# A decode block on one core: fewer TensorE products, and two rows of w2 loaded in two transfers

## The chip, the cores and the metric

The kernel runs on one core of a Trainium2 chip. The metric is the device time of one execution in microseconds, as the median of several runs. A profile of one further execution gives its span (from the first to the last instruction) and what each engine and each DMA queue did in it.

## The reference

One token of a transformer block is decoded for a batch of 4. The input `x` is 4 x 1 x 512; there are 32 heads of 128, a cache of 4096 keys and values per head and batch row, and a feed-forward part of width 1792. All data is float32.

```python
xn = _layernorm(x, axis=-1)                                  # no weights
q = (xn @ wq).reshape(B, Sq, H, Dh).transpose(0, 2, 1, 3)
scores = jnp.einsum("bhqd,bhkd->bhqk", q, k_cache) * (Dh ** -0.5)
p = softmax(scores, axis=-1)
o = jnp.einsum("bhqk,bhkd->bhqd", p, v_cache)
attention = o.transpose(0, 2, 1, 3).reshape(B, Sq, H * Dh) @ wo
h = silu(xn @ w1)
return x + attention + h @ w2
```

The two caches are 256 MiB each; `wq` and `wo` are 8 MiB each, `w1` and `w2` 3.5 MiB each. Every byte is read once.

## The kernel before

**Work and buffers.** A block `i` of 32 is four heads of one batch row: 8 MiB of keys and 8 MiB of values, each one DMA of 128 partitions by 64 KiB (partition `p` holds 128 positions of head `p // 32`). There are three buffers of 8 MiB: `kb[0]` and `kb[1]` for keys, `vb` for values. At the start `kb[1]` also holds `w1`, `x` and small tiles (`early`), and `vb` holds `wq`. At the end `vb` holds `wo`, and `kb[1]` holds `w2` and small tiles (`late`).

**Order.** Everything is written out by hand. Each engine has its own instruction stream, and the class `Queue` counts what an engine has done: `done` raises the engine's semaphore, `wait` makes another engine wait for a count. `load` (line 163 in the trace) issues a DMA and returns what its landing will count. SP issues all the large loads in one order: `w1`, `wq`, the keys of block 0; the keys of block 1 when `h` is out of `kb[1]`; the values of block 0 when the query projection has read `wq` out of `vb` (`p_q`); then keys and values by turns, each when its buffer is free (`k_free`, `v_free`); the last values into `kb[0]`; `wo` in two halves into `vb`; `w2` in five pieces into `kb[1]`. ACT issues the load of `x` and the store of the output.

**Start.** VectorE computes the layer norm. TensorE puts `x` into the accumulator `acc` (`accumulate`, line 239), transposes the normed rows into `xpad`, which is padded to 32 columns, and multiplies by `w1` (line 259) and `wq` (line 273). ACT applies silu, VectorE transposes `h` into `hT` (line 267). The queries are scaled (line 279), spread over the partitions by 32 small products with `heads` (line 286), and copied into `q_col` (line 295).

**Loop.** For each block VectorE multiplies keys by the query (line 358) and adds up halves that GpSimd has added (lines 378 and 353), and finds the smallest per head; ACT takes exponentials and their sums (line 390); TensorE multiplies by the values into `o_ps` (`values`, line 408), ACT copies (line 398), and `collect` (line 419) puts the result into column `i` of `o_t`.

**End.** When the last values are collected, VectorE multiplies the sums by `quad` (line 444), four products with `ones` add them up (line 455), and their reciprocal `rl` is taken (line 461). `o_t` is transposed (line 464), permuted by a product (line 468), and multiplied by `rl` into `xo`, padded to 32 columns (line 474). 32 products with `wo` go into `ow`, 512 columns wide, in four strips of 32 rows by turns (line 487). A row `f` of `w2` means 512 columns for each of the 128 partitions; there are 14 rows, and the first 7 go into `ow` the same way (line 493). ACT copies `ow` to `os` (line 498). Rows 7 to 13 go into `acc` in four products of 128 columns each (`accumulate`), and four products with `pick` add the strips of `os` to it. The last row comes in two halves (`sides`); after each half two blocks of `acc` are done and are copied out by ACT (line 517) and VectorE (line 522). The pieces of `w2` are set by these lines:

```python
W2_CUTS = (7, 11)                       # rows 0-6, 7-10, 11-12, then the two halves of row 13
f_edges = (0, *W2_CUTS, FC - 1)
for name, a, z in zip(("wq", "w2a", "w2b"), f_edges[:-1], f_edges[1:]):
    got_w2.append(load(sp, name, w2_t[:, a:z], w2_p[:, a:z], (k_free, T)))
```

Of the kernel before, what the change touches and what calls it, by code (L numbers as in the profile page):

```python
# [15 lines left out]
G = 4  # L16
# [3 lines left out]
W2_CUTS = (7, 11)  # L20
# [25 lines left out]
def kernel(  # L46
# [11 lines left out]
    nc = tc.nc  # L58
# [13 lines left out]
    scale = float(Dh) ** -0.5  # L72
    xf = x.rearrange("b s d -> (b s) d")
# [20 lines left out]
    q_all = small([P, NQ, G, Dh], "q_all")  # L94
    heads = small([P, NQ, 4, NQ, B], "heads")
# [6 lines left out]
    quad = small([P, G, 4], "quad")  # L102
    perm = small([P, P], "perm")
    ones = small([P, 1], "ones")
    rl = small([P, B], "rl")
    nmean = small([B, 1], "nmean")
    var = small([B, 1], "var")
    rstd = small([B, 1], "rstd")
    t1 = small([B, 1], "t1")
# [16 lines left out]
    x_sb, xc, sq, xn = (early[:B, at + n * D : at + (n + 1) * D] for n in range(4))  # L126
    h_sb = early[:, at + 4 * D : at + 4 * D + FJ]
# [4 lines left out]
    lt = late[:, FC * D : (FC + 1) * D].rearrange("p (b n g) -> p b n g", b=B, n=N)  # L132
    y_t = late[:, (FC + 1) * D : (FC + 1) * D + P].rearrange("p (b h) -> p b h", b=B)
    xo = late[:, (FC + 4) * D : (FC + 4) * D + PH * PH].rearrange("p (r m) -> p r m", r=PH)
# [8 lines left out]
    with tc.tile_critical():  # L143
# [5 lines left out]
        names = ["x", "w1", "wq", "k0", "k1", "v", "v_last", "w2a", "w2b", "w2c", "w2d"]  # L149
# [11 lines left out]
        def load(q, name, to, of_, *needs):  # L161
            q.wait(*needs)
            q.eng.dma_start(to, of_).then_inc(landed[name], 16)  # L163
            loads[name] += 1
            return landed[name], 16 * loads[name]
# [3 lines left out]
        got_x = load(act, "x", x_sb, xf)  # L169
# [14 lines left out]
        nc.vector.memset(xpad, 0.0).then_inc(s_free, 1)  # L184
        nc.vector.memset(q_col[:, T:, :], 0.0).then_inc(s_free, 1)
        nc.vector.memset(heads, 0.0)
# [38 lines left out]
        for u in range(NQ):  # L225
            t = nc.vector.tensor_copy(
                heads[:, u, :, u, :], ident.rearrange("p (j e) -> p j e", j=4)[:, :, :B]
            )
        d_pick = dve.done(
            nc.vector.tensor_reduce(  # L230
                quad,
                ident.rearrange("p (g m) -> p g m", g=G)[:, :, None, :].to_broadcast([P, G, 4, PH]),
                axis=AX, op=ALU.add,
            )
        )
# [10 lines left out]
        pe.wait(c_ident, got_x)  # L246
        accumulate(ident[:B, :B], x_sb, start=True)
        pe.wait(d_xn)
        xt = ps_b[:, : DC * B].rearrange("p (c b) -> p c b", c=DC)
        xn_c = xn.rearrange("b (p c) -> b c p", c=DC)  # L250
        for c in range(DC):
            t = nc.tensor.transpose(xt[:, c, :], xn_c[:, c, :], ident[:B, :B])
        p_xt = pe.done(t)
        dve.wait(p_xt)
        d_xpad = dve.done(nc.vector.tensor_copy(xpad[:, :, :B], xt))
# [12 lines left out]
        pe.wait(got_wq)  # L268
        for c in range(DC):
            for j in range(4):  # L270
                for u in range(NQ):
                    h = HJ * j + G * u
                    t = nc.tensor.matmul(  # L273
                        ps_q[32 * j : 32 * j + 32, u, :], xpad[:, c, :],
                        wq_t[:, c, h * Dh : (h + G) * Dh], start=(c == 0), stop=(c == DC - 1),
                    )
        p_q = pe.done(t)
        dve.wait(p_q)
        d_q = dve.done(nc.vector.tensor_scalar_mul(  # L279
                q_all.rearrange("p u g d -> p (u g d)"), ps_q.rearrange("p u n -> p (u n)"), -scale,  # L280
            ))
        pe.wait(d_q, d_pick)
        for g in range(G):
            for a in range(4):
                for u in range(NQ):
                    t = nc.tensor.matmul(
                        ps_b[32 * g : 32 * g + 32, 32 * a : 32 * a + 32],
                        q_all[:, u, g, 32 * a : 32 * a + 32],
                        heads[:, u].rearrange("p j v b -> p (j v b)"),
                        start=(u == 0), stop=(u == NQ - 1),  # L290
                    )
        p_col = pe.done(t)
        dve.wait(p_col)
        d_col = dve.done(
            nc.vector.tensor_copy(q_col[:, :T, :], ps_b.rearrange("p (a i) -> p i a", a=4))
        )


        got_k[1] = load(sp, "k1", kb[1], cache(k_cache, 1), p_h, d_h, p_xt)
# [17 lines left out]
        for name, a, z in zip(("wq", "w2a", "w2b"), f_edges[:-1], f_edges[1:]):  # L317
            got_w2.append(load(sp, name, w2_t[:, a:z], w2_p[:, a:z], (k_free, T)))
# [109 lines left out]
        with nc.tensor.Fori(0, T - 1) as i:  # L428
# [4 lines left out]
        take(nc.tensor, weights_ready)  # L433
# [3 lines left out]
        p_o = v_free, T  # L437


        pool.wait((k_free, T))  # L440
        c_xo = pool.done(nc.gpsimd.memset(xo, 0.0))
        dve.wait((v_free, T))
        d_lt = dve.done(
            nc.vector.tensor_tensor(  # L444
                lt,
                sums.rearrange("p (n b) -> p b n", b=B)[:, :, :, None].to_broadcast([P, B, N, G * 4]),
                quad.rearrange("p g q -> p (g q)")[:, None, None, :].to_broadcast(
                    [P, B, N, G * 4]
                ),
                op=ALU.mult,  # L450
            )
        )
        pe.wait(d_lt)
        for b in range(B):
            t = nc.tensor.matmul(
                ps_a[:, b : b + 1],
                lt[:, b].rearrange("p n g -> p (n g)"), ones, start=True, stop=True,
            )
        p_l = pe.done(t)
        dve.wait(p_l)  # L460
        d_rl = dve.done(nc.vector.reciprocal(rl, ps_a[:, :B]))
        dve.wait(p_o)
        d_y = dve.done(
            nc.vector.transpose(y_t, o_t.rearrange("p (n b) g -> p b n g", b=B))
# [4 lines left out]
                ps_b, perm, y_t.rearrange("p b r -> p (b r)"), start=True, stop=True,  # L469
            )  # L470
        )
        dve.wait(p_x, d_rl, c_xo)
        d_x = dve.done(
            nc.vector.tensor_tensor(
                xo[:, :, :B], ps_b.rearrange("p (b r) -> p r b", b=B),
                rl[:, None, :].to_broadcast([P, PH, B]), op=ALU.mult,
            )
        )
# [3 lines left out]
        pe.wait(d_x)  # L482
        for n, (a, z) in enumerate(zip(edges[:-1], edges[1:])):
            pe.wait(got_wo[n])
            for r in range(a, z):
                j = 32 * (r % 4)
                nc.tensor.matmul(
                    ow[j : j + 32, :], xo[:, r, :], wo_t[:, r, :], start=(r < 4), stop=False
                )
        pe.wait(d_h, got_w2[0])  # L490
        for f in range(f_edges[1]):
            j = 32 * (f % 4)
            t = nc.tensor.matmul(
                ow[j : j + 32, :], hT[:, f, :], w2_t[:, f, :], start=False,
                stop=(f >= f_edges[1] - 4),
            )
        act.wait(pe.done(t))
        a_os = act.done(nc.scalar.activation(os, ow, AF.Copy))
        for n, (a, z) in enumerate(zip(f_edges[1:-1], f_edges[2:])):
            pe.wait(got_w2[n + 1])  # L500
            for f in range(a, z):
                accumulate(hT[:, f, :B], w2_t[:, f, :])
            if n == 0:
                pe.wait(a_os)
                accumulate(pick[:, :B], os)


        for n, side in enumerate(sides):
            j = 2 - 2 * n
            pe.wait(got_side[n])  # L510
            p_acc = pe.done(
                accumulate(hT[:, FC - 1, :B], w2_t[:, FC - 1, :], stop=True, blocks=(j, j + 1))
            )
# [7 lines left out]
            d_out = dve.done(  # L521
                nc.vector.tensor_copy(  # L522
                    res[:, (j + 1) * P : (j + 2) * P], acc[32 * (j + 1) : 32 * (j + 1) + B, :]
                )
            )
# [35 lines left out]
```

## Time and profile before

| | |
|---|---|
| median of 3 runs | 1302.8 us (1302.73 to 1303.46) |
| profiled execution: time | 1303.4 us |
| profiled execution: span | 1300.5 us |
| busy: PE, DVE, ACT, POOL | 361.1, 964.9, 110.2, 580.9 us |
| DMA | 561.07 MB, mean 431 GB/s |
| mean granted TensorE clock | 0.623 |

In the profile PE is TensorE's products and PEld its weight loads, DVE is VectorE, POOL is GpSimd, SP issues DMAs, and L163 is line 163 of the kernel. A product in float32 appears as two MATMUL records. The granted clock is the TensorE clock that the throttle let through, as a share of full speed. The DMA share is the mean busy share of the core's 16 DMA engines; a DMA is cut into packets, and a packet of 4 bytes closes an engine's part of a transfer. A row of the timeline has start, duration, engine, line, operation, tiles and count, and in brackets the idle time before it and what ended it.

### The profile page before, as it was taken

To read this page: it belongs to the slowest core of one execution; us is meant where nothing else is said; L and a number is where in the kernel's file an instruction comes from. 1 tells how busy PE (TensorE), PEld (TensorE's weight loads), DVE (VectorE), ACT (ScalarE), POOL (GpSimd) and SP (SyncE) were. 2 spreads that over 40 slices of the span, in tenths; PEclk is the share of its full clock that TensorE was granted. 3 is DMA by queue.
4 is the path that set the end of the run, shared out by engine and by line. 5 is a ranking of instruction groups with operands and counts; after the bars stand their busy time and mean duration, and the time that the engine had idled before them with its cause. 6 is when DMAs were issued, how large, how long until landed. Compare 5 with 4: busy or idle time off the path is not lost. (4 is left out here: it accounts for less than half of the span.)

```text
span 1300.5 us, 7378 instructions
## 1 busy us (share of the span) xinstructions
PE 361.1 (28%) x2628; PEld 113.3 (9%) x2628; DVE 964.9 (74%) x449; ACT 110.2 (8%) x311; POOL 580.9 (45%) x137
## 2 busy tenths in 40 slices
PE   2221233321233221123322132332123332113337
PEld 0100001000000000000000000100000000001002
DVE  2499877887777887777797777788777788777770
ACT  1010101001010100101000010100101010010100
POOL 0255534554444554443555443455444455444350
PEclk8755666655666655666665566665566665566668
DMA  9999999999999999999999999999999999999998
GB/s 403 450 422 440 429 441 427 435 435 423 447 423 447 423 445 425 441 429 439 427 437 433 425 445 423 447 423 447 423 443 427 439 429 441 427 431 439 423 433 358
DMA packets 10533, 561.07 MB, mean 431 GB/s; under 512 B 1176, under 2 KB 1432, under 8 KB 1568
## 3 DMA queue, kind: packets, MB, share of 16 engines
q1 hardware_dynamic: 10512, 560.99, 99.6%
q8 instruction: 3, 0.05, 0.0%
q10 hardware_dynamic: 16, 0.02, 0.0%
q14 instruction: 2, 0.02, 0.0%
HBM read 561.00 MB, written 0.01 MB: 431 GB/s over the span
## 5 line engine op out<-in xcount | busy, mean ns | idle before, releaser
L378 POOL TENSOR_TENSOR k<-k 128x2048 f32<-128x2048 f32 x128 | 578.7, 4532 | 676.8 <-POOLq L326 676.8
L358 DVE TENSOR_TENSOR k<-k,q_b 128x4096 f32<-128x4096 f32 x128 | 562.4, 4414 | 226.2 <-DVEq L326 226.1
L408 PE MATMUL o_ps<-v,p_t 128*16 128x512 f32 x1984 | 285.0, 739 | 867.1 <-PEq L326 867.1
L353 DVE TENSOR_REDUCE s<-k 128x32 f32<-128x2048 f32 x128 | 290.8, 2272 | 17.9 <-DVEq L326 17.9
L408 PEld LDWEIGHTS o_ps<-v,p_t 128*16 128x16 f32 x1984 | 67.1, 113 | 1059.2 <-issue 1059.2
L398 ACT ACTIVATE o_sb<-o_ps 128x512 f32<-128x512 f32 x32 | 19.1, 597 | 1010.2 <-ACTq L326 1010.2
L329 DVE COPY q_of<-q_col 128x4 f32 (+1 forms) x33 | 84.8, 2571 | 0.0
L390 ACT ACTIVATE p_t<-s,gm 32x128 f32<-32x128 f32 x128 | 65.9, 515 | 46.0 <-ACTq L326 43.9
L419 PE MATMUL o_t<-pick,o_sb 128*128 128x4 f32 x256 | 33.6, 254 | 33.3 <-PEq L326 33.3
L419 PEld LDWEIGHTS o_t<-pick,o_sb 128*128 128x128 f32 x256 | 31.0, 191 | 62.6 <-issue 62.6
L390 ACT ACT_TABLE_LOAD x16 | 20.5, 1283 | 98.4 <-ACTq L326 98.4
L390 ACT ACTIVATION_READ_ACCUMULATOR p_t<-s,gm x128 | 24.9, 195 | 0.0
L279 DVE TENSOR_SCALAR q_all<-ps_q 128x1024 f32<-128x1024 f32 x1 | 1.2, 1224 | 20.6 <-PE ps_q L273 20.6
L444 DVE TENSOR_TENSOR k<-sums,quad 128x512 f32<-128x512 f32 x1 | 0.7, 693 | 19.0 <-PE o_t L419 19.0
L333 DVE STREAM_TRANSPOSE q_b<-q_of 128x128 f32<-128x128 f32 x33 | 10.8, 327 | 4.9
L367 DVE TENSOR_REDUCE m<-s 128x1 f32<-128x128 f32 x32 | 9.2, 286 | 4.7
L273 PE MATMUL ps_q<-v,xpad 128*32 128x512 f32 x64 | 8.8, 706 | 13.3 <-DMA v<-in_A_wq_dram 13.3
L408 PE MATMUL o_ps<-k,p_t 128*16 128x512 f32 x64 | 9.5, 757 | 8.3 <-DMA k<-in_A_v_cache_dram 8.3
L369 DVE STREAM_TRANSPOSE mt<-m 128x32 f32<-128x32 f32 x32 | 6.8, 212 | 4.7
L522 DVE COPY k<-acc 4x128 f32<-4x128 f32 x2 | 0.6, 286 | 12.5 <-PE acc L239 12.5
L371 DVE TENSOR_REDUCE gm<-mt 128x1 f32<-128x32 f32 x32 | 6.0, 186 | 4.7
L267 DVE STREAM_TRANSPOSE hT<-k 128x448 f32<-128x448 f32 x1 | 0.9, 939 | 10.3 <-ACT k L265 10.3
(62 smaller groups left out, 54.1 us busy)
## 6 DMA issues: line engine op xcount, KB each, us to landing
v<-in_A_wo_dram SPq DMA_DIRECT2D x2, 4096.0 KB, 27.2
k<-in_B_w_dram SPq DMA_DIRECT2D x1, 3584.0 KB, 11.2
k<-in_B_w_dram SPq DMA_DIRECT2D x1, 1792.0 KB, 30.3
k<-in_B_w_dram SPq DMA_DIRECT2D x1, 1024.0 KB, 32.4
k<-in_A_k_cache_dram SPq DMA_DIRECT2D x32, 45.4
k<-in_B_w_dram SPq DMA_DIRECT2D x1, 512.0 KB, 33.2
v<-in_A_v_cache_dram SPq DMA_DIRECT2D x31, 27.2
k<-in_B_w_dram SPq DMA_DIRECT2D x2, 128.0 KB, 33.0
```

The lines of the kernel that those rows point to most:

```text
L273: t = nc.tensor.matmul(ps_q[32 * j : 32 * j + 32, u, :], xpad[:, c, :], wq_t[:, c, h * Dh : (h + G) * Dh], start=(c == 0), stop=(c == DC - 1),
L329: nc.vector.tensor_copy(q_of, q_col[:, at, :].rearrange("p i g -> p (i g)")).then_inc(spread_done, 1)
L333: nc.vector.transpose(q_b[:, n, :], q_of[:, :, None].to_broadcast([P, G, PH])).then_inc(spread_done, 1)
L353: nc.vector.tensor_reduce(s[:, a:z], k[:, a:z, : Dh // 2], axis=AX, op=ALU.add).then_inc(summed, 1)
L358: nc.vector.tensor_tensor(k[:, a:z, :], k[:, a:z, :], q_b[:, n, None, :].to_broadcast([P, z - a, Dh]), op=ALU.mult,).then_inc(products, 1)
L367: nc.vector.tensor_reduce(m_t, s, axis=AX, op=ALU.min).then_inc(summed, 1)
L369: nc.vector.transpose(mt, m_t.to_broadcast([P, PH])).then_inc(summed, 1)
L378: nc.gpsimd.tensor_tensor(kb[n][:, a:z, : Dh // 2], kb[n][:, a:z, : Dh // 2], kb[n][:, a:z, Dh // 2 :], op=ALU.add,).then_inc(halves, 1)
L390: t = nc.scalar.activation(p_t[rows, :, g], s_t[n][rows, :], AF.Exp, bias=gm[n][rows, :], scale=-1.0, accum_out=sums[rows, bass.ds(i * 2 + ...
L398: nc.scalar.activation(o_sb.rearrange("p r d -> p (r d)"), o_ps, AF.Copy).then_inc(rows_ready, 1)
L408: t = nc.tensor.matmul(o_ps[j : j + NR * G, :], p_t[:, rows, :].rearrange("p r g -> p (r g)"), v[:, rows, :].rearrange("p r d -> p (r d)") ...
L419: t = nc.tensor.matmul(to, o_sb[:, r, :], pick[:, r * G : (r + 1) * G], start=(r == 0), stop=(r == NR - 1),)
```

## The change

- **Query path.** `x` lies in rows 8 to 11 of a zeroed tile `x_sb` of 32 rows, whose load now waits for the zeroing. The layer norm runs on 32 rows. `xpad` is made by four VectorE transposes instead of TensorE's. The order of columns in `wq`'s products changes; their result is transposed by VectorE straight into `q_t` (in `vb`, where `wq` was) and scaled into `q_col`. The 32 products with `heads` and `q_all` are gone. The first values are therefore loaded after `d_col` instead of `p_q`.
- **Sums.** One product with a square of ones gives the sums to all partitions; it and the reciprocal now stand between the last exponentials and the last values. `o_t` is multiplied by `rl` before its transpose, and `xo` is a plain copy, with 4 columns instead of 32 for each product.
- **x in the output.** `x` is written into the strips of `ow` at the start, with zeros in the other rows, instead of into `acc` by products; `add_x` in place of `pick` picks it up with the strips.
- **w2.** Its pieces are now rows 0 and 1, 2 to 7, 8 to 11, 12, and the two halves of row 13. Rows 0 and 1 come in two transfers: partitions 116 to 127, then partitions 0 to 115. Rows 0 to 11 all go into `ow`, so ACT copies `ow` after row 11; only rows 12 and 13 go into `acc`.

TensorE has 58 products fewer. The core of the diff:

```diff
-W2_CUTS = (7, 11)
+W2_CUTS = (2, 8, 12)
+PART = 116
+X_ROW = 8
...
+    rows_x = slice(X_ROW, X_ROW + B)
...
+    q_t = vb.rearrange("p r d -> p (r d)")[:, : T * PH].rearrange("p (m e) -> p m e", e=PH)
...
-        got_x = load(act, "x", x_sb, xf)
+        c_x = dve.done(nc.vector.memset(x_sb, 0.0))
+        got_x = load(act, "x", x_sb[rows_x], xf, c_x)
...
-        pe.wait(c_ident, got_x)
-        accumulate(ident[:B, :B], x_sb, start=True)
-        pe.wait(d_xn)
...
+        dve.wait(d_xn)
+        xn_c = xn.rearrange("b (m e c) -> b m c e", m=4, c=DC)
+        for m in range(4):
+            t = nc.vector.transpose(xpad[PH * m : PH * (m + 1)], xn_c[:, m])
...
-        d_q = dve.done(nc.vector.tensor_scalar_mul(
-                q_all.rearrange("p u g d -> p (u g d)"), ps_q.rearrange("p u n -> p (u n)"), -scale,
-            ))
-        pe.wait(d_q, d_pick)
...
+        d_qt = dve.done(
+            nc.vector.transpose(q_t, ps_q.rearrange("p u (m e) -> p (u m) e", e=PH))
+        )
+        dve.wait(d_qt)
         d_col = dve.done(
...
+        nc.vector.tensor_copy(ow[:PH], x_sb)
+        nc.vector.memset(ow[PH : 2 * PH], 0.0)
+        d_ow = dve.done(nc.vector.memset(ow[2 * PH :], 0.0))
...
-            load(sp, "v", vb, cache(v_cache, i), p_q if i == 0 else (v_free, i))
+            load(sp, "v", vb, cache(v_cache, i), d_col if i == 0 else (v_free, i))
...
-        for name, a, z in zip(("wq", "w2a", "w2b"), f_edges[:-1], f_edges[1:]):
-            got_w2.append(load(sp, name, w2_t[:, a:z], w2_p[:, a:z], (k_free, T)))
+        for name, a, z in zip(("w2e", "wq", "w2a", "w2b"), f_edges[:-1], f_edges[1:]):
+            parts = ((PART, P), (0, PART)) if a == 0 else ((0, P),)
+            for b, e in parts:
+                got = load(sp, name, w2_t[b:e, a:z], w2_p[b:e, a:z], (k_free, T))
+            got_w2.append(got)
...
-        take(nc.tensor, weights_ready)
+        p_w = pe.done(nc.tensor.wait_ge(weights_ready, 1))
+        dve.wait(p_w)
+        d_lt = dve.done(
...
+        p_l = pe.done(
+            nc.tensor.matmul(
+                ps_b, ones, lt.rearrange("p t g -> p (t g)"), start=True, stop=True
+            )
+        )
+        dve.wait(p_l)
+        d_rl = dve.done(nc.vector.reciprocal(rl.rearrange("p t g -> p (t g)"), ps_b))
         nc.tensor.wait_ge(landed["v_last"], 16)
         values(kb[(T - 2) % 2])
...
-                    ow[j : j + 32, :], xo[:, r, :], wo_t[:, r, :], start=(r < 4), stop=False
-                )
-        pe.wait(d_h, got_w2[0])
-        for f in range(f_edges[1]):
...
+                    ow[j : j + B, :], xo[:, :, r], wo_t[:, r, :], start=(r < 4), stop=False
+                )
+        pe.wait(d_h)
+        rows = f_edges[-2]
+        for n, (a, z) in enumerate(zip(f_edges[:-2], f_edges[1:-1])):
+            pe.wait(got_w2[n])
+            for f in range(a, z):
+                j = 32 * (f % 4)
+                t = nc.tensor.matmul(
+                    ow[j : j + B, :], hT[:, f, rows_x], w2_t[:, f, :], start=False,
+                    stop=(f >= rows - 4),
+                )
         act.wait(pe.done(t))
         a_os = act.done(nc.scalar.activation(os, ow, AF.Copy))
...
+        pe.wait(got_w2[-1])
+        for f in range(rows, f_edges[-1]):
+            accumulate(hT[:, f, rows_x], w2_t[:, f, :], start=(f == rows))
+        pe.wait(a_os, d_add)
+        accumulate(add_x, os)
```

More of the change, by code (lines that the diff above doesn't have):

```diff
@@ L93 @@
     hT = small([P, FC, PH], "hT")
-    q_all = small([P, NQ, G, Dh], "q_all")
-    heads = small([P, NQ, 4, NQ, B], "heads")
+    x_sb = small([PH, D], "x_sb")
     q_col = small([P, T + 1, G], "q_col")
@@ L101 @@
     pick = small([P, NR * G], "pick")
-    quad = small([P, G, 4], "quad")
+    add_x = small([P, B], "add_x")
     perm = small([P, P], "perm")
[L104 to L109, printed above, removed]
+    quad = small([P, G], "quad")
+    ones = small([P, P], "ones")
+    nmean = small([PH, 1], "nmean")
+    var = small([PH, 1], "var")
+    rstd = small([PH, 1], "rstd")
+    t1 = small([PH, 1], "t1")
     small([P, -(CONST_AT + taken) % 256 // 4 + 64], "fill")
@@ L125 @@
     at = DC * F
-    x_sb, xc, sq, xn = (early[:B, at + n * D : at + (n + 1) * D] for n in range(4))
-    h_sb = early[:, at + 4 * D : at + 4 * D + FJ]
+    xc, sq, xn = (early[:PH, at + n * D : at + (n + 1) * D] for n in range(3))
+    h_sb = early[:, at + 3 * D : at + 3 * D + FJ]
     wq_t = vb.rearrange("p (c m) d -> p c (m d)", c=DC)
+    q_t = vb.rearrange("p r d -> p (r d)")[:, : T * PH].rearrange("p (m e) -> p m e", e=PH)
     wo_t = vb.rearrange("p r d -> p (r d)").rearrange("p (r n) -> p r n", n=D)
@@ L131 @@
     w2_t = late[:, : FC * D].rearrange("p (f n) -> p f n", f=FC)
-    lt = late[:, FC * D : (FC + 1) * D].rearrange("p (b n g) -> p b n g", b=B, n=N)
-    y_t = late[:, (FC + 1) * D : (FC + 1) * D + P].rearrange("p (b h) -> p b h", b=B)
-    xo = late[:, (FC + 4) * D : (FC + 4) * D + PH * PH].rearrange("p (r m) -> p r m", r=PH)
+    lt = late[:, FC * D : FC * D + T * G].rearrange("p (t g) -> p t g", g=G)
+    rl = late[:, FC * D + P : FC * D + 2 * P].rearrange("p (t g) -> p t g", g=G)
+    o_n = late[:, FC * D + 2 * P : FC * D + 3 * P].rearrange("p (t g) -> p t g", g=G)
+    y_t, xo = (
+        late[:, (FC + n) * D : (FC + n) * D + B * PH].rearrange("p (b r) -> p b r", b=B)
+        for n in (1, 4)
+    )
     ow = ps_q[:, 0, :]
@@ L183 @@
         c_zero = pool.done(nc.gpsimd.memset(p_t, 0.0))
-        nc.vector.memset(xpad, 0.0).then_inc(s_free, 1)
-        nc.vector.memset(q_col[:, T:, :], 0.0).then_inc(s_free, 1)
-        nc.vector.memset(heads, 0.0)
+        nc.vector.memset(q_col[:, T:, :], 0.0).then_inc(s_free, 2)
         c_ops = dve.done(nc.vector.memset(o_ps, 0.0))
@@ L224 @@
         nc.vector.tensor_copy(perm, ident.rearrange("p (q h) -> p h q", q=4))
-        for u in range(NQ):
-            t = nc.vector.tensor_copy(
-                heads[:, u, :, u, :], ident.rearrange("p (j e) -> p j e", j=4)[:, :, :B]
-            )
         d_pick = dve.done(
             nc.vector.tensor_reduce(
-                quad,
-                ident.rearrange("p (g m) -> p g m", g=G)[:, :, None, :].to_broadcast([P, G, 4, PH]),
-                axis=AX, op=ALU.add,
-            )
+                quad, ident.rearrange("p (g m) -> p g m", g=G), axis=AX, op=ALU.add,
+            )
+        )
+        dve.wait(d_pick)
+        d_add = dve.done(
+            nc.vector.tensor_add(add_x, pick[:, :B], ident[:, rows_x])
         )
@@ L243, in accumulate @@
             return last
-        pe.wait(c_ident, got_x)
-        accumulate(ident[:B, :B], x_sb, start=True)
-        pe.wait(d_xn)
[L249 to L255, printed above, removed]
+        dve.wait(d_xn)
+        xn_c = xn.rearrange("b (m e c) -> b m c e", m=4, c=DC)
+        for m in range(4):
+            t = nc.vector.transpose(xpad[PH * m : PH * (m + 1)], xn_c[:, m])
+        d_xpad = dve.done(t)
         pe.wait(d_xpad, got_w1)
@@ L268 @@
         pe.wait(got_wq)
+        wq_g = wq_t.rearrange("p c (n g d) -> p c n g d", g=G, d=Dh)
         for c in range(DC):
@@ L271 @@
                 for u in range(NQ):
-                    h = HJ * j + G * u
                     t = nc.tensor.matmul(
                         ps_q[32 * j : 32 * j + 32, u, :], xpad[:, c, :],
-                        wq_t[:, c, h * Dh : (h + G) * Dh], start=(c == 0), stop=(c == DC - 1),
+                        wq_g[:, c, G * u : G * u + G, j, :], start=(c == 0), stop=(c == DC - 1),
                     )
@@ L278 @@
         dve.wait(p_q)
-        d_q = dve.done(nc.vector.tensor_scalar_mul(
-                q_all.rearrange("p u g d -> p (u g d)"), ps_q.rearrange("p u n -> p (u n)"), -scale,
-            ))
-        pe.wait(d_q, d_pick)
[L283 to L293, printed above, removed]
+        d_qt = dve.done(
+            nc.vector.transpose(q_t, ps_q.rearrange("p u (m e) -> p (u m) e", e=PH))
+        )
+        dve.wait(d_qt)
         d_col = dve.done(
-            nc.vector.tensor_copy(q_col[:, :T, :], ps_b.rearrange("p (a i) -> p i a", a=4))
-        )
-        got_k[1] = load(sp, "k1", kb[1], cache(k_cache, 1), p_h, d_h, p_xt)
+            nc.vector.tensor_scalar_mul(
+                q_col[:, :T, :].rearrange("p (n b) a -> p n b a", b=B),
+                q_t.rearrange("p (n a) e -> p n e a", a=G)[:, :, rows_x, :], -scale,
+            )
+        )
+        nc.vector.tensor_copy(ow[:PH], x_sb)
+        nc.vector.memset(ow[PH : 2 * PH], 0.0)
+        d_ow = dve.done(nc.vector.memset(ow[2 * PH :], 0.0))
+        got_k[1] = load(sp, "k1", kb[1], cache(k_cache, 1), p_h, d_h)
         for i in range(T - 1):
@@ L436 @@
         collect(o_t[:, T - 1, :])
[L437 to L462, printed above, removed]
+        dve.wait(d_rl, (v_free, T))
+        t = dve.done(nc.vector.tensor_tensor(o_n, o_t, rl, op=ALU.mult))
+        dve.wait(t)
         d_y = dve.done(
-            nc.vector.transpose(y_t, o_t.rearrange("p (n b) g -> p b n g", b=B))
+            nc.vector.transpose(y_t, o_n.rearrange("p (n b) g -> p b n g", b=B))
         )
@@ L468 @@
             nc.tensor.matmul(
-                ps_b, perm, y_t.rearrange("p b r -> p (b r)"), start=True, stop=True,
+                ps_a[:, :P], perm, y_t.rearrange("p b r -> p (b r)"), start=True, stop=True
             )
         )
[L472 to L482, printed above, removed]
+        dve.wait(p_x)
+        d_x = dve.done(nc.vector.tensor_copy(xo.rearrange("p b r -> p (b r)"), ps_a[:, :P]))
+        pe.wait(d_x, d_ow)
         for n, (a, z) in enumerate(zip(edges[:-1], edges[1:])):
@@ L487 @@
                 nc.tensor.matmul(
-                    ow[j : j + 32, :], xo[:, r, :], wo_t[:, r, :], start=(r < 4), stop=False
+                    ow[j : j + B, :], xo[:, :, r], wo_t[:, r, :], start=(r < 4), stop=False
                 )
-        pe.wait(d_h, got_w2[0])
-        for f in range(f_edges[1]):
[L492 to L496, printed above, removed]
+        pe.wait(d_h)
[7 more added lines that the diff above has]
+                    stop=(f >= rows - 4),
+                )
         act.wait(pe.done(t))
         a_os = act.done(nc.scalar.activation(os, ow, AF.Copy))
[L499 to L505, printed above, removed]
+        pe.wait(got_w2[-1])
[3 more added lines that the diff above has]
+        accumulate(add_x, os)
         for n, side in enumerate(sides):
```

11 lines of the change are left out of this document (9 added, 2 removed).

## The prediction

> **What bounds the kernel now.** I read the page's slices and queues first, then the chain that ended last, then narrow windows over the end.
>
> ```profile
> span 1300.5 us, 7378 instructions
> DMA  9999999999999999999999999999999999999998
> DMA packets 10533, 561.07 MB, mean 431 GB/s; under 512 B 1176, under 2 KB 1432, under 8 KB 1568
> q1 hardware_dynamic: 10512, 560.99, 99.6%
> q10 hardware_dynamic: 16, 0.02, 0.0%
> ```
>
> The sixteen DMA engines are busy for 99.6% of the span, in every slice. No compute engine bounds anything before the last slice, and the bytes are the same after the change. So only two things can move the time: a hole in the stream, or its end.
>
> ```profile
> 1262.59 32.40 DMA k<-in_B_w_dram
> 1295.03 2.12 PE acc L239 x60
> 1297.18 0.29 DVE k L522
> k<-in_B_w_dram SPq DMA_DIRECT2D x1, 1792.0 KB, 30.3
> k<-in_B_w_dram SPq DMA_DIRECT2D x1, 1024.0 KB, 32.4
> k<-in_B_w_dram SPq DMA_DIRECT2D x1, 512.0 KB, 33.2
> k<-in_B_w_dram SPq DMA_DIRECT2D x2, 128.0 KB, 33.0
> 1262.21 2.23 SPq L163 DMA_DIRECT2D k<-in_B_w_dram  x5
> v<-in_A_wo_dram SPq DMA_DIRECT2D x2, 4096.0 KB, 27.2
> 1260.72 0.80 SPq L163 DMA_DIRECT2D v<-in_A_wo_dram  x2
> ```
>
> The chain (start, us, what) ends in the five w2 loads. They are issued from 1262.21, some 0.43 us apart, so with the times to landing they land at 1292.5, 1295.0, 1296.3, 1296.6 and 1296.9; wo's second half, issued at 1261.1, lands at 1288.3. After the last landing there remain two products, two copies and the output's transfer. The profiled time is 1303.4 us, 2.9 more than the span; the median of three is 1302.8, and I add the sum to that.
>
> ```profile
> core 0: us, PE busy (x) PEld busy (x) DVE busy (x) ACT busy (x) POOL busy (x), PEclk, DMA share, GB/s
> 1292.00:1294.00 2.00, 2.00 (x23) 0.59 (x18) 0.00 (x0) 0.00 (x0) 0.00 (x0) 1.00 0.99 414
> 1295.00:1295.20 0.20, 0.17 (x8) 0.17 (x12) 0.00 (x0) 0.20 (x1) 0.00 (x0) 1.00 0.80 287
> 1295.60:1295.80 0.20, 0.20 (x17) 0.20 (x9) 0.00 (x0) 0.00 (x0) 0.00 (x0) 1.00 0.19 67
> 1295.80:1296.40 0.60, 0.60 (x24) 0.32 (x16) 0.00 (x0) 0.00 (x0) 0.00 (x0) 1.00 0.20 70
> 1296.40:1296.60 0.20, 0.20 (x12) 0.20 (x9) 0.00 (x0) 0.00 (x0) 0.00 (x0) 1.00 0.08 26
> ```
>
> These windows show how the stream ends. Full until about 1295.0; then engines run dry one by one; a share of 0.20 is three of sixteen, and these three work until about 1296.5, some 0.9 us after the other thirteen. Also, 414 GB/s at a share of 0.99 is 26.1 GB/s per engine, while 70 GB/s on three engines is 23: an engine does not speed up when its neighbours stop. Each engine is a server of its own, and the end is set by the one that was given most.
>
> **The change: the split load (decides).** Two rows of w2, 4 KB per partition, go from one even transfer into transfers of 12 and of 116 partitions. How are partitions dealt to engines? The page's counts tell: 10512 packets on q1 are 73 transfers of 128 data packets and 16 closing ones. The 16 packets on q10 are the two transfers of four rows (x and the output): four data and four closing packets each. So 128 partitions go to 16 engines in equal shares of 8, and four go to four engines, one each. Equal shares in both. I take it that shares stay equal, with as many engines as allow it: 12 partitions on 12 engines, and 116 = 4 x 29 on only four, which are among the twelve if both start from the same engine.
>
> [...]
>
> A 4 KB packet takes 4.096/26.1 = 0.157 us. Before, these two rows cost every engine 8 packets (1.26 us). After, four engines carry 29 + 1 = 30: 22 x 0.157 = 3.4 us more. The others carry one or none, 1.1 to 1.3 us less. All later pieces are dealt evenly and keep that order. If the four belong to the thirteen early engines, the latest of them ended near 1295.7 and the last landing moves by 3.4 - 0.9 = 2.5 us, to 1299.4; if one of the three late ones is among them, by 3.4. Drawn blindly it would be so in 6 of 10 cases, but the lateness is that of one execution. I take 2.5 and keep 3.4 for the range.
>
> **The pieces, and what PE and ACT do at the end.** The other w2 pieces are 6, 4, 1 and two half rows, where they were 7, 4, 2 and two halves: the bytes behind the four-row piece fall from 3 rows to 2 (about 1.3 us). The four-row piece now belongs to the 512-wide products into `ow`, so `ow` is complete only after it, and copied then; before, the copy came after the first piece, under the last ones.
>
> ```profile
> 1269.04 9.46 PE L408 MATMUL o_ps<-k,p_t 128*16 128x512 f32 x64 [8.35 <-DMA k<-in_A_v_cache_dram]
> 1270.72 0.17 PEld L408 LDWEIGHTS o_ps<-k,p_t 128*16 128x16 f32 x4 [0.68 <-issue]
> 1275.33 0.11 PEld L408 LDWEIGHTS o_ps<-k,p_t 128*16 128x16 f32 x4 [0.32 <-issue]
> 1284.74 8.46 PE L487 MATMUL ps_q<-v,k 128*32 128x512 f32 x64 [0.38 <-DVE k L474]
> 1294.98 0.60 ACT L498 ACTIVATE k<-ps_q 128x512 f32<-128x512 f32 x1 [15.71 <-PE ps_q L493]
> 1297.18 0.60 DVE L522 COPY k<-acc 4x128 f32<-4x128 f32 x2 [12.49 <-PE acc L239]
> ```
>
> A product is two matmul records. Four weight loads, two 512-wide products, take 0.17 + 0.68 = 0.85 us at half clock and 0.43 at full: 0.43 and 0.21 each. With the last landing at 1299.4, the six-row piece lands near 1295.7 (four rows, 8 x 8 KB per engine, are 2.4 us) and the four-row piece at 1298.1.
>
> At full clock: four products to 1299.05 with their drain, the ACT copy (0.60 and two waits of about 0.1) to 1299.85, then four `add_x` products and four side products, 16 records at 2.12/60 = 0.035, to 1300.4; DVE's second copy starts near 1300.6. Before it started at 1297.48. That is +3.1: the copy's chain costs 0.6 over the 2.5 of the transfer.
>
> But the clock is unlikely to hold:
>
> ```profile
> core 0: us, PE busy (x), PEclk, DMA share, GB/s
> 1256.87:1260.28 3.41, 2.37 (x25) 1.00 1.20 519
> 1277.35:1280.76 3.41, 2.18 (x20) 1.00 0.98 423
> 1280.76:1284.18 3.42, 2.48 (x10) 0.50 1.00 431
> 1284.18:1287.59 3.41, 3.03 (x17) 0.50 0.90 389
> 1287.59:1291.00 3.41, 3.41 (x36) 1.00 0.97 407
> ```
>
> PE busy 2.37 of a 3.41 us window kept the full clock, 2.18 did not, and it took a nearly full window to win it back. In the changed kernel PE ends the wo products near 1291.8 (16 of them, 0.21 each, need wo's second half), does the two split rows at about 1292.1 to 1292.6, and then waits some 3.1 us for the six-row piece. A window that holds most of that gap loses the clock. Then six products take 2.6 us instead of 1.3 (to 1298.3), four take 1.7 (to 1300.1), and copy and small products end near 1301.8: +4.3.
>
> [...]
>
> I take **+4.2 us**: 2.5 from the four engines, 0.6 from the copy's chain, 1.1 from the clock (1.2 at the half clock, a little less for a part regained).
>
> **What costs nothing, and its cover.** The 58 products less are in the early projection, the setup and the last accumulation.
>
> ```profile
> 12.34 5.91 PE L259 MATMUL ps_a<-k,xpad 128*32 128x448 f32 x32 [4.39 <-DMA k<-in_B_w_dram]
> 18.89 0.94 DVE L267 STREAM_TRANSPOSE hT<-k 128x448 f32<-128x448 f32 x1 [10.32 <-ACT k L265]
> 40.38 1.22 DVE L279 TENSOR_SCALAR q_all<-ps_q 128x1024 f32<-128x1024 f32 x1 [20.55 <-PE ps_q L273]
> 52.05 8.75 DVE L358 TENSOR_TENSOR k<-k,q_b 128x4096 f32<-128x4096 f32 x2 [7.47 <-DVEq L326]
> 40.38 0.33 SPq L163 DMA_DIRECT2D v<-in_A_v_cache_dram  x1
> 85.04 0.33 SPq L163 DMA_DIRECT2D k<-in_A_k_cache_dram  x1
> ```
>
> The memset that x now waits for (about 0.5 us) lies under the 4.39 us for which PE waits for w1; if x were 4.4 us late, PE would start late, and k1 be issued later, with k0 still in flight to 51. The first V load waits on SP for `d_col` instead of `p_q`: a 128x1024 transpose (0.94 x 1024/448 = 2.1 us) and a scale (0.3 to 1.2), so it is issued at about 43.5 instead of 40.4. Queued behind it on SP is the third K load (issued at 85), ahead of it in the engines are the rest of k0 and all of k1, 8 MB at 431 GB/s, until about 70: no hole. DVE's new writes to `ow` (three, about 1.5 us) lie under its 7.47 us of waiting for k0. The weights' sum and reciprocal move ahead of the last values, under the 8.35 us in which PE waits for them; wo's products start earlier and then wait for wo's second half. SP issues one transfer more, 0.43 us, under some 26 us of queue.
>
> **The rivals.**
> - *The clock holds.* The gap could fall across two windows, neither of them idle enough. +3.1, 1305.9. For it: the 2.37 row; against it the 2.18 one. Chance 0.20.
> - *The 116 are dealt 8 to an engine* (fourteen engines with 8, one with 4, one with none; twelve others one more). That agrees with both counts on the page too. Then no engine gets more than 0.16 us more, the pieces land as before, the copy's chain costs 0.6 and the clock up to 1.2: +0.2 to +2.0, likely +0.8, 1303.6, within 0.2%: the rival that ends on the other side, not slower. It decides as soon as no engine carries over 19 of the 4 KB packets (11 more than before, 1.7 us: 0.9 of lead plus the 0.8 that measurement cannot tell with the chain's 0.6 and noise). [...] Chance 0.16.
> - *Bandwidth is a pool*, and the four engines go faster once twelve are dry: the last landing stays at 1296.9, and only the chain's +0.6 to +1.8 is left, 1304. The 23 GB/s per engine with three left speaks against it. Chance 0.03.
> - *The late engines are those relieved* under the second rival, and the tail's products fit: -0.3 to -1.0, about 1302.2. A saving over 2.6 us would need more than the 1.5 us from first to last dry engine; chance 0.02, which I put on the side of faster.
>
> **How the numbers follow.** Four engines and a lost clock, my forecast: 0.59, giving +3.6 (clock half regained) to +5.3 (a late engine among the four); it and the first rival are 0.79. A measurement of this kernel tells about 0.2%, 2.6 us. Of the 0.79, about 0.09 lies below +2.6 (the four among the earliest, the clock kept); with the second rival and the pool that makes 0.28 for no change, 0.02 for faster and 0.70 for slower. The forecast is 1302.8 + 4.2 = 1307.0. The main cases alone would span 1305.2 to 1308.4; to leave out no more than 2 in 10 the range reaches down to the second rival's likely value, and up to the late engine with its clock lost: 1303.5 to 1308.4.
>
> **What would show it.** Right: the load of 116 partitions is the slow one; the DMA share falls near 1295 to about 0.25 (four engines) and stays there for 3 to 4 us, where it was 0.20 for 0.9; the last piece lands near 1299.4; PEclk is 0.50 around 1296; ACT's copy of `ow` starts after 1299 and the output's transfer some 4 us later than 1297.9. Wrong: a share that falls as before within 1.6 us of 1295 (dealt 8 to an engine); a tail at 0.25 with over 150 GB/s (a pool); PEclk 1.00 throughout (the clock's term); or any drop of the share before 1290 (a hole that I cover at nothing).

## The result, and the profile after

The changed kernel takes 1311.4 us (1310.17 to 1312.05, 6 runs) against 1302.87 us (6 runs): a ratio of 1.0065, with a 95% interval of 1.0055 to 1.0075. It is 8.5 us slower, where +4.2 was forecast; the way was right, and the time lies outside the range of 1303.5 to 1308.4. The profiled execution took 1310.44 us, with a span of 1308.7.

From the page of the changed kernel: the span, the DMA slices, the counts and the DMA queues.

```profile
span 1308.7 us, 7159 instructions
DMA  9999999999999999999999999999999999999996
DMA packets 10677, 561.07 MB, mean 429 GB/s; under 512 B 1192, under 2 KB 1448, under 8 KB 1712
q1 hardware_dynamic: 10656, 560.99, 99.3%
```

Only the last slice differs: there is no hole before it. On q1 there are 144 packets more. There are still 73 transfers of 128 partitions, since the pieces behind the first two rows are five as before; the transfers of 12 and of 116 come on top. They bring 128 data packets and 16 closing ones, and 16 = 12 + 4: twelve engines carried the 12 partitions, and four the 116. An 8-to-an-engine deal would have closed on 15 engines instead of 4, 155 packets more.

The end of the stream in the changed kernel, in windows (start:end, length, busy times and counts by engine, PEclk, DMA share, GB/s):

```profile
core 0: us, PE busy (x) PEld busy (x) DVE busy (x) ACT busy (x) POOL busy (x), PEclk, DMA share, GB/s
1287.00:1289.00 2.00, 0.00 (x0) 0.00 (x0) 0.00 (x0) 0.00 (x0) 0.00 (x0) 1.00 0.94 242
1291.00:1293.00 2.00, 2.00 (x16) 0.50 (x12) 0.00 (x0) 0.00 (x0) 0.00 (x0) 0.50 1.05 240
1293.00:1295.00 2.00, 1.81 (x16) 0.22 (x8) 0.00 (x0) 0.00 (x0) 0.00 (x0) 0.97 0.92 229
1295.00:1297.00 2.00, 0.87 (x4) 0.10 (x4) 0.00 (x0) 0.00 (x0) 0.00 (x0) 1.00 0.97 380
1299.00:1301.00 2.00, 1.50 (x10) 0.38 (x12) 0.00 (x0) 0.00 (x0) 0.00 (x0) 0.74 0.25 107
1302.40:1302.80 0.40, 0.40 (x8) 0.19 (x4) 0.00 (x0) 0.00 (x0) 0.00 (x0) 0.50 0.07 23
```

The last two rows are the forecast picture: a plateau at 0.25, four engines of sixteen, until the stream ends at 1302.8 (at 1296.6 before, by the row that the prediction quoted). The first three rows were not forecast. All sixteen engines are busy, yet together they move about 240 GB/s where the kernel before moved 414: some 15 GB/s per engine instead of 26. That lasts until about 1295, and then the rate returns.

The chain that ended last, in the changed kernel (start, us, what):

```profile
1262.88 36.58 DMA k<-in_B_w_dram
1299.51 4.47 PE ps_q L483 x20
1303.99 0.61 ACT k L488
1304.64 0.64 PE acc L243 x16
1305.31 0.29 DVE k L510
```

The six-row piece lands at 1299.5, not 1295.7. Behind it come, as forecast, six and four products, ACT's copy of `ow`, eight small products and the output's copies. These begin at 1305.31, 8.13 us later than the 1297.18 of before.

### The profile page after: what moved, and what is told of

It is laid out like the page before. It is cut to its first block, busy times and chain, and to the rows that moved or that the text cites. A ratio compares the mean times of both kernels' runs of the same rounds, so it can differ in the third digit from the quotient of the medians.

```text
span 1308.7 us, 7159 instructions
## 1 busy us (share of the span) xinstructions
PE 359.8 (27%) x2516; PEld 108.4 (8%) x2516; DVE 968.4 (74%) x454; ACT 110.2 (8%) x311; POOL 580.3 (44%) x136
## 5 line engine op out<-in xcount | busy, mean ns | idle before, releaser
L474 PE MATMUL ps_q<-v,k 128*4 128x512 f32 x64 | 8.9, 710 | 4.9 <-DMA v<-in_A_wo_dram 4.5
L258 PE MATMUL ps_a<-k,xpad 128*32 128x448 f32 x32 | 5.9, 912 | 14.6 <-DVE xpad L253 14.6
```

The source lines that it names most:

```text
L474: nc.tensor.matmul(ow[j : j + B, :], xo[:, :, r], wo_t[:, r, :], start=(r < 4), stop=False)
```

## The experiments

**Which edit costs: the split undone, and the split alone.** "Joined" is the changed kernel with rows 0 and 1 in one transfer:

```diff
-            parts = ((PART, P), (0, PART)) if a == 0 else ((0, P),)
+            parts = ((0, P),)
```

> The changed kernel with rows 0 and 1 of w2 in one transfer of 128 partitions; all else as changed. If the two transfers are what costs (theory A): the last landing is back near 1296.9, and only the tail's two terms stay, the copy chain (0.6) and a lost clock (up to 1.2): 1303.5 to 1304.7. If another edit costs (rival: a hole at the start, the longer wait of the first V load, the pieces): 1306 or more, with a dip of the DMA share before 1285.

Measured: 1303.43 us against 1302.70 (10 and 19 runs), ratio 1.0006 [0.9997, 1.0016]. The stream is at its full rate where the changed kernel was slow:

```profile
core 0: us, PE busy (x) PEld busy (x) DVE busy (x) ACT busy (x) POOL busy (x), PEclk, DMA share, GB/s
1289.00:1291.00 2.00, 1.88 (x20) 0.54 (x24) 0.00 (x0) 0.00 (x0) 0.00 (x0) 1.00 0.98 418
```

With "before and split", the split is put into the kernel before:

```diff
+        for p0, p1 in ((116, P), (0, 116)):
+            got_e = load(sp, "w2e", w2_t[p0:p1, :2], w2_p[p0:p1, :2], (k_free, T))
-        for name, a, z in zip(("wq", "w2a", "w2b"), f_edges[:-1], f_edges[1:]):
+        for name, a, z in zip(("wq", "w2a", "w2b"), (2, *f_edges[1:-1]), f_edges[1:]):
...
-        pe.wait(d_h, got_w2[0])
+        pe.wait(d_h, got_e, got_w2[0])
```

> The kernel before with one edit: the first piece of w2 comes as rows 0 and 1 of partitions 116 to 127, rows 0 and 1 of partitions 0 to 115, and rows 2 to 6. Theory A: the last landing moves as in the changed kernel, by 6.3 us, and the tail behind it does not grow, since the copy of ow still hangs on the first piece and rows 7 to 13 behind it take 1.9 us to land on the four engines: 1302.9 + 6.3 = 1309.2, 1308 to 1310.5. With the packet time that the prediction used (0.157 us) it would be 1305.4. Rival, other edits carry the loss: under 1304.

Measured: 1310.05 us (4 runs), ratio 1.0057 [1.0040, 1.0074]. The slow stretch is back, at the same place:

```profile
core 0: us, PE busy (x) PEld busy (x) DVE busy (x) ACT busy (x) POOL busy (x), PEclk, DMA share, GB/s
1289.00:1291.00 2.00, 2.00 (x24) 0.55 (x20) 0.00 (x0) 0.00 (x0) 0.00 (x0) 1.00 0.99 253
```

The split carries the loss: +7.35 alone, while all the other edits together are +0.73, which the interval of the joined run does not tell from nothing. The time is 0.85 over the expected 1309.2, which the interval does not tell from nothing. The tail was expected not to grow, and in the trace it does: the output copies begin at 1305.26, some 2.5 us after the stream's end at 1302.7, where in the kernel before they began 0.6 after it; PEclk is 0.50 from 1299 to 1303.

**Is a transfer on four engines slow by itself?** The 116 partitions go last, behind the half rows:

```diff
-            parts = ((PART, P), (0, PART)) if a == 0 else ((0, P),)
+            parts = ((PART, P),) if a == 0 else ((0, P),)
...
+        got_w2[0] = load(sp, "w2e", w2_t[:PART, : f_edges[1]], w2_p[:PART, : f_edges[1]])
```

> The changed kernel with the transfer of 116 partitions issued last of all, behind the half rows; TensorE takes up w2 only after it, so the tail is longer by some 4 us of products, and only the stream's end is to be read. If its packets are slow because other engines write at the same time (theory B): they run nearly alone here, the share falls to 0.25 at about 100 GB/s, which is 26 GB/s per engine, for 3 to 4 us, and the last landing comes at 1299 to 1300. If a transfer of 116 partitions on four engines is slow by itself (theory C): about 60 GB/s at the same share, and the last landing near 1302.5.

Its windows at the end (one execution, 1311.14 us, with the long tail that the text above foresaw):

```profile
core 0: us, PE busy (x) PEld busy (x) DVE busy (x) ACT busy (x) POOL busy (x), PEclk, DMA share, GB/s
1296.20:1297.00 0.80, 0.00 (x0) 0.00 (x0) 0.00 (x0) 0.00 (x0) 0.00 (x0) 0.96 0.25 102
1297.00:1299.00 2.00, 0.00 (x0) 0.00 (x0) 0.00 (x0) 0.00 (x0) 0.00 (x0) 0.50 0.24 98
1299.00:1301.00 2.00, 0.98 (x8) 0.26 (x12) 0.00 (x0) 0.00 (x0) 0.00 (x0) 0.50 0.02 8
```

98 GB/s at a share of 0.24 is 25.5 GB/s per engine, and the stream ends before 1300. The same packets go at full speed: alone, the transfer costs what the prediction gave it. It was slow only beside other engines' transfers (theory B; C falls).

**Overload, or what is written where?** Two other cuts. The cut at 112 gives 16 and 112 partitions, which divide among all sixteen engines:

```diff
-PART = 116
+PART = 112
```

> The changed kernel with the cut at partition 112 in place of 116: two transfers still, of 16 and 112 partitions, which equal shares put on all sixteen engines (1 and 7 packets each). If the uneven deal is the cause: as the joined kernel within 0.5, thus 1303.5 to 1305. If cutting into two transfers is the cause, or a partition count that is not 128: as the changed kernel, 1310 or more. Something between, 1305 to 1308, would mean that engines in each other's partitions cost without any overload: 7 packets at 0.28 instead of 0.157 us are 0.9 us more on every engine.

Measured: 1305.67 us against 1302.70 (10 and 19 runs), ratio 1.0023 [1.0013, 1.0033]: the case in between. The cut at 120:

```diff
-PART = 116
+PART = 120
```

> The changed kernel with the cut at partition 120: transfers of 8 and of 120 partitions. Equal shares put 120 on 15 engines, 8 packets each, so 15 engines and then 8 count as carriers and none is overloaded by more than one packet. Theory D: shares of 8 neighbouring partitions do not agree with the partitions that an engine serves in a transfer of 128, so it costs like the cut at 112, which measured 2.2 us over the joined kernel: 1305 to 1306.5. If only the overload of four engines cost: 1303.5.

Measured, in one execution: 1305.99 us against 1302.46 beside it. The page's counts, of the cut at 112 and then of that at 120:

```profile
q1 hardware_dynamic: 10672, 560.99, 99.5%
```

```profile
q1 hardware_dynamic: 10663, 560.99, 99.5%
```

Above the 10512 of before these are 160 = 128 + 16 + 16 and 151 = 128 + 8 + 15, as equal shares give. (The rival deal, in which each engine takes a sixteenth of the partitions, rounded up, would count the same here; only the cut at 116 tells the two apart.) No engine is overloaded in either by more than one packet, yet the cut at 112 costs 2.2 us more than the joined kernel. The windows of the cut at 112 while the pieces load:

```profile
core 0: us, PE busy (x) PEld busy (x) DVE busy (x) ACT busy (x) POOL busy (x), PEclk, DMA share, GB/s
1287.00:1289.00 2.00, 2.00 (x16) 0.30 (x8) 0.00 (x0) 0.00 (x0) 0.00 (x0) 0.60 1.08 291
1289.00:1291.00 2.00, 1.06 (x12) 0.22 (x12) 0.00 (x0) 0.00 (x0) 0.00 (x0) 1.00 1.02 274
```

Busy engines at two thirds of the rate, without overload; in the cut at 120 it is 193 GB/s from 1287 to 1289. So the slowing is no matter of four engines having too much. Theory D's premise, that a share of 7 or 8 partitions is not the one that its engine serves in a transfer of 128, was not shown.

**The disputed cost by itself.** The joined kernel gets 480 KB more, six transfers of four partitions and 20 KB a partition, all on the same four engines: the first run's plateau below has a share of 0.24. The first run writes partitions 0 to 15 and eight of 32 to 45; the second, 64 to 79 and eight of 96 to 109; the third does as the second, but reads what the first read. The author took the first set to be the four engines' own in a transfer of 128, and the second to be that of four other engines. By theory D nothing is then slowed in the first run, and eight engines are in the other two. Which engine serves which partition was not shown.

```diff
+                for s in (0, 1, 2, 3, 32, 33):            # second and third: (64, 65, 66, 67, 96, 97)
+                    got_more = load(
+                        sp, "more", late[s : s + 13 : 4, 11264:],
+                        cache(k_cache, 0).rearrange("p r d -> p (r d)")[s : s + 4, 11264:],
+                    )                                     # third: [s - 64 : s - 60, 11264:]
```

> The joined kernel with 480 KB more, loaded and not used: behind rows 0 and 1 of w2, six transfers of four partitions and 20 KB each (from the keys into free columns), which go to the same four engines. [...] Theory D, an engine that writes partitions which another engine serves is slowed with it: nothing is slowed here; the four engines carry 6 x 0.76 = 4.6 us more, the other twelve run dry as before (share 0.25 from about 1296.5), GB/s stays above 400 until 1295, last landing near 1301. Rival E, any overload of four engines slows all: 1303 or later, with 250 GB/s at full share on the way.

> [...] Theory D: the 20 KB packets and those of the other four engines run at about half speed while both last, about 330 GB/s at full share from 1289 to 1296; the four engines need up to 9 us instead of 4.6, last landing 1304 to 1306. Rival E and a rival in which the reads of the source collide: as the run with its own partitions, within 0.5 us.

> The run with foreign partitions, but reading exactly what the run with its own partitions read, so that only the partitions written differ between those two. Theory D (what is written where): as with foreign partitions, last landing 1306 to 1307.5, about 200 GB/s at full share, time 1313 to 1315. If the addresses read made the difference: as with its own partitions, last landing near 1301, time 1307.

Measured, in one execution each: 1307.28, 1314.25 and 1313.12 us; the kernel before took 1302.46 beside the first two and 1302.88 beside the third. Windows of the first:

```profile
core 0: us, PE busy (x) PEld busy (x) DVE busy (x) ACT busy (x) POOL busy (x), PEclk, DMA share, GB/s
1289.00:1291.00 2.00, 2.00 (x16) 0.46 (x12) 0.00 (x0) 0.00 (x0) 0.00 (x0) 0.50 1.05 449
1291.00:1293.00 2.00, 2.00 (x16) 0.39 (x12) 0.00 (x0) 0.00 (x0) 0.00 (x0) 0.73 0.92 391
1297.00:1299.00 2.00, 1.73 (x12) 0.30 (x12) 0.00 (x0) 0.00 (x0) 0.00 (x0) 1.00 0.24 97
```

And of the third:

```profile
core 0: us, PE busy (x) PEld busy (x) DVE busy (x) ACT busy (x) POOL busy (x), PEclk, DMA share, GB/s
1289.00:1291.00 2.00, 2.00 (x24) 0.54 (x20) 0.00 (x0) 0.00 (x0) 0.00 (x0) 1.00 1.05 219
1291.00:1293.00 2.00, 2.00 (x16) 0.30 (x8) 0.00 (x0) 0.00 (x0) 0.00 (x0) 1.00 1.01 205
1295.00:1297.00 2.00, 0.00 (x0) 0.00 (x0) 0.00 (x0) 0.00 (x0) 0.00 (x0) 0.59 0.94 197
```

Between these two only the partitions written differ. The first keeps the full rate and has its 4.6 us as a plateau at 0.25: overload alone costs its bytes and no more. The third moves 200 GB/s with all engines busy. The trace, which has the time of every packet, shows it packet by packet: each 12 KB packet of the six-row piece takes 460 ns in the first run, as in the joined kernel, and 926 to 985 ns in the third when it starts between 1289.5 and 1296. So what is written where decides, and E falls. Theory D was too mild: it gave 330 GB/s, since by the author's assumption only eight engines share partitions.

Which partitions each engine wrote stands in no trace here. The runs show that the partitions written decide (449 and 391 GB/s in the first run, 219 and 205 in the third), and that others must be transferring at the time (25.5 GB/s per engine for the 116 alone); that an engine is held up by the one that serves the same partitions was not shown.

**How far does it reach?** As the third run, with two partitions in each of the six transfers instead of four, and so on two engines: from 1303 to 1305 the share is 0.13, at 48 GB/s. By the author's assumption these write the partitions of two others, and the remaining twelve share none; why engines without a share in it slowed in the third run was the open question.

```diff
-                        sp, "more", late[s : s + 13 : 4, 11264:],
+                        sp, "more", late[s : s + 5 : 4, 11264:],
```

> [...] If only the sharing engines slow (pairs): 12 x 26 + 4 x 13 = 364 GB/s at full share from 1289 to 1293. If any such pair slows all sixteen alike: about 200 GB/s. If it goes by the number of pairs: near 290.

```profile
core 0: us, PE busy (x) PEld busy (x) DVE busy (x) ACT busy (x) POOL busy (x), PEclk, DMA share, GB/s
1291.00:1293.00 2.00, 2.00 (x22) 0.51 (x16) 0.00 (x0) 0.00 (x0) 0.00 (x0) 1.00 0.97 199
1295.00:1297.00 2.00, 0.00 (x0) 0.00 (x0) 0.00 (x0) 0.00 (x0) 0.00 (x0) 1.00 1.02 201
```

The time is 1313.24 us in one execution, with half the extra bytes of the third run. Two engines that write partitions of this set halve all sixteen: 12.5 GB/s each. No engine is spared, for every 12 KB packet that starts between 1289.5 and 1296 takes 940 to 1006 ns instead of 460. It does not go by how many engines write so: from 1291 to 1293 the third run's four left 205 GB/s, and these two 199. Through what the other engines are held back, no run here shows.

**The tail's two terms.** The changed kernel was run once more, and beside it with products that are not used, to keep TensorE at work:

```diff
+            for f in range(10 if n == 0 else 0):
+                j = 32 * (f % 4)
+                nc.tensor.matmul(
+                    ps_a[j : j + B, :], hT[:, 0, rows_x], w2_t[:, 0, :FJ], start=True, stop=True,
+                )
```

> The changed kernel once more, unchanged, beside the next one: 1311.4, within 1310 to 1312.

> The changed kernel with ten more 448-wide products, whose result is not used, behind the two split rows, where TensorE waits for the next piece. If the lost clock costs what the prediction gave it (1.2 us): PEclk stays at 1.00 to the end, and the time is 0.8 to 1.4 less than the unchanged one beside it. If the tail hangs on landings alone: the same within 0.3.

Measured: 1310.85 us (1310.38 to 1311.50) and 1309.78 us (1309.55 to 1310.14), 4 runs each. Windows of the second:

```profile
core 0: us, PE busy (x), PEclk, DMA share, GB/s
1296.00:1298.00 2.00, 1.81 (x16) 0.84 0.88 345
1298.00:1300.00 2.00, 2.00 (x12) 0.50 0.31 126
1300.00:1302.00 2.00, 2.00 (x17) 0.80 0.26 99
1302.00:1304.00 2.00, 1.50 (x32) 1.00 0.03 12
```

The time falls by 1.07, within what was expected, but not quite as expected. The clock did drop, since the added products stand behind a wait of their own, and it came back before 1302, under the last products; in the changed kernel it is 0.50 there, by the row of 1302.40 above. That supports the clock's term; how much of the 1.07 is the clock and how much the landings of that execution, these runs do not separate.

The last version copies `ow` early, with joined rows:

```diff
-W2_CUTS = (2, 8, 12)
+W2_CUTS = (5, 9, 12)
...
-        rows = f_edges[-2]
+        rows = f_edges[2]
...
+        pe.wait(a_os, d_add)
+        accumulate(add_x, os, start=True)
+        for n in (2, 3):
```

> The joined kernel with w2 in the pieces rows 0 to 4, 5 to 8, 9 to 11, 12 and the two halves; rows 0 to 8 go into ow, which is copied while rows 9 to 12 land, and add_x comes ahead of them. The stream ends as in the kernel before (1296.9), the tail loses the copy's chain and a little of the backlog of products: 0.6 to 0.9 less than the joined kernel, thus 1302.3 to 1302.8, not slower than the kernel before. If the joined kernel's loss has another cause: 1303.4 again.

Measured: 1302.90 us against 1302.88 (11 and 15 runs), ratio 1.0001 [0.9992, 1.0010]. Beside the joined kernel's +0.73 that is 0.7 less, of the size expected of the copy's chain; but the two intervals do not tell the 0.7 from nothing, and the pieces of w2 differ too. It is as fast as the kernel before, not better; no version here beats it beyond what can be measured.

## Why the prediction was right or wrong

**Right.** The stream's end decides: there is no hole in any slice. The first V load was issued at 42.89 (about 43.5 forecast), and its cover held. Equal shares: 12 on twelve engines and 116 on four. The plateau at 0.25 came. So did the order of the tail and, within noise, its price: 8.13 us between the output copies of before and after, less the 3.8 us by which the six-row piece came later than forecast (1299.5 for 1295.7), leaves 4.3, the sum that the prediction gave with the clock lost. The copy's chain, put at 0.6, fits the 0.7 above, which is within noise. The clock was lost later than forecast, and on a shorter gap. It was to be 0.50 around 1296, where the row of 1295.00 above has 1.00; it fell at about 1300:

```profile
core 0: us, PE busy (x) PEld busy (x) DVE busy (x) ACT busy (x) POOL busy (x), PEclk, DMA share, GB/s
1298.00:1300.00 2.00, 0.49 (x8) 0.17 (x10) 0.00 (x0) 0.00 (x0) 0.00 (x0) 0.99 0.32 131
1300.00:1302.00 2.00, 2.00 (x14) 0.27 (x10) 0.00 (x0) 0.00 (x0) 0.00 (x0) 0.50 0.23 91
```

TensorE's wait for the six-row piece, in the timeline:

```profile
1299.51 4.44 PE L483 MATMUL ps_q<-k,hT 128*4 128x512 f32 x20 [2.35 <-DMA k<-in_B_w_dram]
```

The gap was 2.35 us, not 3.1, and the clock fell all the same. That the sum of the tail came out so close is in part luck.

**Wrong: the price of a packet.** The step that failed is "A 4 KB packet takes 4.096/26.1 = 0.157 us". The 26.1 GB/s came from windows of transfers of 128 partitions, each dealt to the engines in the same shares of eight. The six-row piece landed 3.8 us later than forecast; so by an estimate the 116 partitions took that much more on their four engines than the forecast 29 x 0.157 = 4.6, thus some 8.4, or 0.29 us a packet. The packets in the trace agree: those of 4 KB took 159 ns each in the kernel before, in the changed kernel 264 in the median and up to 464, and they end at 1295.1, 8.7 us after the first starts. The other engines' packets were slowed with them: those of 12 KB took 460 ns at the least and 736 in the median. The stream's end moved by 6.2 (1296.6 to 1302.8), where 2.5 was taken: 3.7 of the 4.3 us between forecast and measurement. The rest no run here separates.

**Why it was not seen.** The prediction read from the row at 70 GB/s that an engine does not get faster when its neighbours stop, and concluded that each is a server of its own. The row supports only the one direction. It says nothing of a transfer of another number of partitions beside the full stream, and no row at the end of the kernel before could: the 73 transfers on its q1 are all of 128. The mechanism that failed is thus that each engine serves its packets by itself, whatever the others write. The cost had a floor from the bytes and no upper bound. An unknown of this kind, a new pattern of writing beside a full stream, should have had a rival of its own, with the range reaching up to it. The upper end of the range, 1308.4, also lies a little above the largest case shown (+5.3, thus 1308.1); neither reaches 1311.4.

**The rivals.** The 8-to-an-engine deal is refuted by the count of closing packets where the cut is at 116: 144 packets more in the changed kernel, not 155. The pool is refuted by the plateau at 107 GB/s. That the clock holds fell with PEclk at 0.50 from 1300. The late engines that are relieved needed the refuted deal.

## What to carry to other kernels

When a load is cut along partitions, count from its closing packets how many engines carry it (here 12 for 12 partitions, 4 for 116, 16 for 112, 15 for 120), and then measure what the stream moves while it runs beside other loads. In these runs transfers of 116, 112 and 120 partitions slowed the whole stream from 414 GB/s to about 240, 274 and 193 while they ran beside transfers of 128, and small ones into partitions 64 to 79 and 96 to 109 to about 200; small ones into partitions 0 to 15 and 32 to 45 did not (391 to 449). Cut along the free dimension instead, as the joined kernel does at 418 GB/s, or put the odd transfer where nothing else runs (25.5 GB/s per engine). A rate read from one pattern is a price for that pattern alone.

## What the runs showed of the hardware that was not expected

Two engines writing partitions 64 to 71, 96, 97, 100 and 101 brought all sixteen from 414 to about 200 GB/s, with a DMA share that stayed near 1.0: the share does not show it, only GB/s does.

Also, SP's issue of one small load took 7.0 us instead of 0.43 in the changed kernel, as its row for line 170 shows (duration min/median/max in ns):

```profile
L170 SPq DMA_DIRECT2D k<-in_B_w_dram x7: 256/378/7025, 1262.1 to 1271.7; - x7
```

It cost nothing there: it was over at 1271.2, and the first packet of rows 0 and 1 starts at 1286.4. What it waited for, no run shows.
